# Attention decode with a gated MLP on one core: K evacuation on one engine, 32-column score matmuls, running maxima, one K stream with V trailing, deeper buffers

## The chip, the cores and the metric

One core of a Trainium2 chip (trn2). Times are microseconds (us) of device time; medians over the executions of a kernel. Ratios are the mean time of one kernel's fast runs over that of the other's from the same rounds on the same chip, so they are not quite the ratios of the medians that stand beside them.

## The reference, cut to what matters

```python
# x: 1x1x1024; k_cache, v_cache: 1x4x65536x128 (bf16); 32 query heads, 8 per K/V head
q = (x @ wq)                                    # wq 1024x4096
p = softmax(q k^T / sqrt(128)); o = p v         # over 65536 positions, 4 K/V heads
a = o @ wo                                      # wo 4096x1024
z = gelu(x @ w_in); ...; b = (z1 * g) @ w_out   # w_in 1024x3584, w_out 1792x1024
out = g * a + (1 - g) * b                       # 1x1x1024
```

K and V are 67 MB each. All the rest that is read is 28 MB. Every byte is used once, so the kernel reads 162 MB and does little arithmetic on each.

## The kernel before

K arrives in blocks of 4096 positions (1 MB), one transfer each, as [128 partitions, 2, 2048]: on every partition two runs of 4096 bytes. TensorE transposes 8 chunks of 128x128 into a PSUM tile; VectorE and ScalarE in turn copy it to a staging tile; TensorE multiplies it with 8 query columns; VectorE copies 64 chunks of scores into one big SBUF tile. When a head is done, VectorE takes its maximum, ScalarE does the exponentials in place, and V blocks are multiplied with them. (SBUF is the large on-chip memory that the transfers fill, PSUM the one that TensorE writes; an evacuation is a copy out of PSUM; QK is the product of keys and queries, a chunk is 128 positions of it, and a bank is one PSUM tile of scores.)

```python
KN_BUFS = 4; V_BUFS = 5; W_BUFS = 4; WO_BUFS = 2; STG_BUFS = 4
...
cpool, apool, spool, wpool, kpool, vpool, wopool, stpool   # SBUF pools, opened in this order
...                                                        # (each pool follows the one before it)
S_all = spool.tile([P, Hkv, NA, REP, 8], BF16, name="S_all")
...
class KHead:
    def emit_block(self, b, eng):                          # eng is nc.sync
        knat = rr(kpool, "k", KN_BUFS, [P, NSB, R * Dh], BF16)
        eng.dma_start(out=knat[:], in_=A_k_cache[...].rearrange("(sbl p r) d -> p sbl (r d)", p=P, r=R))
        for ...:                                           # 4 groups of 8 transposes
            pt = rr(ppt, "t", PT_BUFS, [P, 8, P], BF16)
            ...                                            # nc.tensor.transpose x8
            if evac_ctr[0] % 2 == 0: nc.vector.tensor_copy(out=stg[:], in_=pt[:])
            else:                    nc.scalar.copy(out=stg[:], in_=pt[:])
            evac_ctr[0] += 1
            ...                                            # QK of the group two back
...
def softmax_stats(g):
    Mg = apool.tile([P, REP], F32, name=f"M{g}")           # 32 bytes per partition, one for each head
    nc.vector.tensor_reduce(out=Mg[:], in_=S_all[:, g]..., op=ALU.max)
...
for g in range(1, Hkv):                                    # head by head
    for b in range(lead): kh.emit_block(b, eng)            # 4 K blocks alone
    softmax_exp(g - 1)
    for b in range(lead, NBLK):                            # 12 pairs of a K and a V block
        kh.emit_block(b, eng); vh.emit_block(vb_idx, eng)
        if vb_idx == wo_at: vh.emit_wo(nc.scalar)          # 2 MB of output weights, ScalarE's queue
        ...
    ...                                                    # 4 V blocks alone, output projection
```

A scheduler orders the instructions of each engine; the order here is close to the one written.

## Time and profile before

Median 424.48 us of 4 runs.

The page's table of 40 slices (10.5 us each), of the kernel before: busy tenths of engines, granted TensorE clock in tenths, mean busy tenths of the 16 DMA engines, and GB/s moved.

```profile
PE   0224998899887998868868888959878888673443
DVE  0001433444654334353433333354332333510000
ACT  1000434455559434516624333436432333250000
PEclk9999859699969769975988887757885888855555
DMA  7999999999989999999999999999999999999991
GB/s 257 412 410 366 418 411 413 399 401 401 372 328 386 407 408 407 406 408 407 399 393 410 406 409 407 409 408 391 404 373 409 405 409 406 407 393 408 408 379 54
```

The DMA is busy from end to end and moves about 407 GB/s, with small dips at the fourth slice (366), at 105 to 126 us (372, 328) and at 305 us (373).

The chain of waits of the kernel before, shares by engine: DMA first.

```profile
DMA 49%; PE 37%; DVE 5%; ACT 4%; issue 2%; SPq 2%; ACTq 0%
```

The groups of instructions that the change touches, before (busy us and mean ns of one behind the count; then idle time before them and what ended it):

```profile
L284 ACT COPY stg<-t 128x1024 bf16<-128x1024 bf16 x128 | 129.0, 1012 | 188.9 <-PE t L274 186.3
L282 DVE COPY stg<-t 128x1024 bf16<-128x1024 bf16 x128 | 88.3, 690 | 126.6 <-PE t L274 125.7
L254 DVE CAST S_all<-qk 128x512 bf16<-128x512 f32 x32 | 22.1, 692 | 38.5 <-PE qk L246 38.2
L299 DVE TENSOR_REDUCE M<-S_all 128x8 f32<-128x4096 bf16 x4 | 17.7, 4417 | 0.1
```

The waits of the DMA queue's own engine (SPq is SyncE's sequencer, which issues K, V and most weights), before; us in total, times, longest.

```profile
SPq L263 <- PE t L274: 115.9, 44, 6.2
SPq L346 <- DMA wo<-in_A_wo_dram: 21.9, 2, 11.0
SPq L133 <- DMA wo<-in_A_wo_dram: 14.5, 1, 14.5
SPq L154 <- DMA wo<-in_A_wo_dram: 13.5, 1, 13.5
```

The first line: the issue of a K block waits for a free K buffer, which is what limits run-ahead. The other three: the issue of query weights, input weights and V waits for the landing of *output* weights. Such sums are time in which SyncE stood still, not time lost: that has to be read from what the DMA did meanwhile.

### The profile page before, as it was taken

The page shows a single profiled execution, that of the slowest core. Times are in us where ns is not written, and L with a number is a line of the kernel's source. Part 1 is how long each engine was busy: PE and PEld are TensorE (multiplying, and loading weights), DVE is VectorE, ACT ScalarE, POOL GpSimd, SP SyncE. Part 2 cuts the span into 40 slices and gives each one's busy share as a digit, 9 for nine tenths or more (in the row PEclk, how much of TensorE's full clock was granted, in tenths as well). Part 3 has the DMA queues.
Part 4 walks back from the last instruction along what each step waited for, and adds up shares of the span by engine and source line. Part 5 has one row for each costly group of instructions (what it writes and reads, how often), then busy time and mean ns, then how long its engine had stood idle before and what let it go on. Part 6 is the DMA issues. An engine that isn't in the chain of part 4 may idle for free.

```text
span 420.6 us, 15057 instructions
## 1 busy us (share of the span) xinstructions
PE 312.6 (74%) x7018; PEld 295.9 (70%) x7018; DVE 138.9 (33%) x232; ACT 156.2 (37%) x198; POOL 2.4 (1%) x12
## 2 busy tenths in 40 slices
PE   0224998899887998868868888959878888673443
PEld 0224898788777997868868877949878888573333
DVE  0001433444654334353433333354332333510000
ACT  1000434455559434516624333436432333250000
POOL 2000000000000000000000000000000000000000
PEclk9999859699969769975988887757885888855555
DMA  7999999999989999999999999999999999999991
GB/s 257 412 410 366 418 411 413 399 401 401 372 328 386 407 408 407 406 408 407 399 393 410 406 409 407 409 408 391 404 373 409 405 409 406 407 393 408 408 379 54
DMA packets 43583, 162.99 MB, mean 388 GB/s; under 512 B 2816, under 2 KB 2816, under 8 KB 42496
## 3 DMA queue, kind: packets, MB, share of 16 engines
q1 hardware_dynamic: 39072, 153.63, 92.3%
q10 hardware_dynamic: 4160, 8.39, 5.4%
q8 instruction: 55, 0.90, 0.9%
q0 software_dynamic: 288, 0.00, 0.1%
q14 instruction: 8, 0.07, 0.0%
HBM read 162.01 MB, written 0.00 MB: 385 GB/s over the span
## 4 chain that ended last, share of the span: by engine, by line
DMA 49%; PE 37%; DVE 5%; ACT 4%; issue 2%; SPq 2%; ACTq 0%
DMA k<-in_A_k_cache_dram 31%; PE t L274 22%; DMA v<-in_A_v_cache_dram 11%; DMA w<-in_A_wq_dram 8%; PE qk L246 6%; PE acc L355 5%; DVE M L299 3%; ACT S_all L320 2%; ACT stg L284 2%; PE outa_ps L388 1%; SPq L346 1%; DVE S_all L254 1%; PE acc L136 0%; SPq L263 0%; PE nm_ps L312 0%
## 5 line engine op out<-in xcount | busy, mean ns | idle before, releaser
L284 ACT COPY stg<-t 128x1024 bf16<-128x1024 bf16 x128 | 129.0, 1012 | 188.9 <-PE t L274 186.3
L274 PE MATMUL t<-ident_b,k 128*128 128x128 bf16 x2048 | 179.3, 254 | 24.9 <-DMA k<-in_A_k_cache_dram 21.5
L274 PEld LDWEIGHTS <-k 128*128 128x128 bf16 x2048 | 150.5, 115 | 27.9 <-DMA k<-in_A_k_cache_dram 23.5
L282 DVE COPY stg<-t 128x1024 bf16<-128x1024 bf16 x128 | 88.3, 690 | 126.6 <-PE t L274 125.7
L355 PE MATMUL acc<-S_all,v 128*128 128x8 bf16 x2048 | 65.3, 175 | 31.7 <-DMA v<-in_A_v_cache_dram 27.8
L246 PE MATMUL qk<-qT,stg 128*128 128x8 bf16 x2048 | 85.6, 168 | 4.3 <-ACT stg L284 2.4
L355 PEld LDWEIGHTS <-v 128*128 128x128 bf16 x2048 | 60.4, 100 | 34.5 <-DMA v<-in_A_v_cache_dram 30.0
L246 PEld LDWEIGHTS <-stg 128*128 128x128 bf16 x2048 | 74.4, 100 | 12.7 <-ACT stg L284 6.5
L254 DVE CAST S_all<-qk 128x512 bf16<-128x512 f32 x32 | 22.1, 692 | 38.5 <-PE qk L246 38.2
L320 ACT ACTIVATE S_all<-S_all,nm 128x512 bf16<-128x512 bf16 x32 | 22.6, 710 | 23.1 <-DVE nm L314 23.1
L136 PE MATMUL acc<-xT,w 128*128 128x1 bf16 x256 | 8.1, 166 | 23.5 <-DMA w<-in_A_wq_dram 23.5
L136 PEld LDWEIGHTS <-w 128*128 128x128 bf16 x256 | 7.4, 104 | 24.1 <-DMA w<-in_A_wq_dram 24.1
L299 DVE TENSOR_REDUCE M<-S_all 128x8 f32<-128x4096 bf16 x4 | 17.7, 4417 | 0.1
L379 DVE TENSOR_TENSOR oT_sb<-acc,rl 128x8 bf16<-128x8 f32 x4 | 0.7, 167 | 44.2 <-PE acc L355 44.2
L303 PE MATMUL mT_ps<-ident_f,M 128*8 128x128 f32 x4 | 1.4, 351 | 11.6 <-DVE M L299 11.6
L146 DVE TENSOR_TENSOR qT_acc<-qT_acc,acc 128x32 f32<-128x32 f32 x7 | 1.3, 188 | 23.9 <-PE acc L136 23.9
L303 PEld LDWEIGHTS mT_ps<-ident_f,M 128*8 128x8 f32 x4 | 0.3, 83 | 12.1 <-DVE M L299 12.1
L388 PEld LDWEIGHTS <-wo 128*128 128x128 bf16 x256 | 7.5, 104 | 1.5 <-issue 1.5
L388 PE MATMUL outa_ps<-oT_sb,wo 128*128 128x1 bf16 x256 | 7.5, 165 | 1.1 <-DVE oT_sb L379 1.0
L157 PE MATMUL acc<-xT,w 128*128 128x1 bf16 x224 | 6.8, 164 | 0.0
L157 PEld LDWEIGHTS <-w 128*128 128x128 bf16 x224 | 6.3, 98 | 0.0
L320 ACT ACTIVATION_READ_ACCUMULATOR S_all<-S_all,nm 128x1 f32 x32 | 6.0, 188 | 0.0
(64 smaller groups left out, 36.5 us busy)
## 6 DMA issues: line engine op xcount, KB each, us to landing
k<-in_A_k_cache_dram SPq DMA_DIRECT2D x64, 1024.0 KB, 15.0
v<-in_A_v_cache_dram SPq DMA_DIRECT2D x64, 1024.0 KB, 14.8
wo<-in_A_wo_dram ACTq DMA_DIRECT2D x4, 2048.0 KB, 18.9
w<-in_A_wq_dram SPq DMA_DIRECT2D x8, 1024.0 KB, 13.6
w<-in_B_w_in_dram SPq DMA_DIRECT2D x8, 896.0 KB, 16.3
w<-in_B_w_out_dram SPq DMA_DIRECT2D x7, 512.0 KB, 13.2
x<-in_A_x_dram SPq DMA_DIRECT2D x1, 2.0 KB
g<-in_gate_w_dram SPq DMA_DIRECT2D x1, 2.0 KB
```

The source lines that it names most:

```text
L136: nc.tensor.matmul(qps[:, h : h + 1], lhsT=wqb[:, h * Dh : (h + 1) * Dh], rhs=xT[:, dc : dc + 1], start=True, stop=True,)
L157: nc.tensor.matmul(zps[:, fi : fi + 1], lhsT=wib[:, fi * P : (fi + 1) * P], rhs=xT[:, dc : dc + 1], start=True, stop=True,)
L246: nc.tensor.matmul(self.qkb[:, cl, :], lhsT=stg[:, j, :], rhs=qT[:, g * REP : (g + 1) * REP], start=True, stop=True,)
L254: nc.vector.tensor_copy(out=S_all[:, g, bank * (CPB // 8) : (bank + 1) * (CPB // 8), :, :], in_=self.qkb[:].rearrange("p (a b) h -> p a h ...
L274: nc.tensor.transpose(out=pt[:, j, :], in_=knat[:, sbl, r * Dh : (r + 1) * Dh], identity=ident_b[:],)
L282: nc.vector.tensor_copy(out=stg[:], in_=pt[:])
L284: nc.scalar.copy(out=stg[:], in_=pt[:])
L299: nc.vector.tensor_reduce(out=Mg[:], in_=S_all[:, g].rearrange("p a h b -> p h a b"), axis=AX.XY, op=ALU.max)
L320: nc.scalar.activation(out=S_all[:, g, :, h, :], in_=S_all[:, g, :, h, :], func=ACT.Exp, bias=nmg[:, h : h + 1], scale=SCALE, accum_out=L[ ...
L346: eng.dma_start(out=vb[:], in_=A_v_cache[0, g, b * BROWS : (b + 1) * BROWS, :].rearrange("(sbl p r) d -> p sbl (r d)", p=P, r=R),)
L355: nc.tensor.matmul(self.oT_ps[:, :REP], lhsT=vb[:, sbl, r * Dh : (r + 1) * Dh], rhs=S_all[:, g, c // 8, :, c % 8], start=(c == 0), stop=(c ...
L388: nc.tensor.matmul(outa_ps[:, jn : jn + 1], lhsT=wo_tiles[gg][:, h, jn * P : (jn + 1) * P], rhs=oT_sb[:, gg * REP + h : gg * REP + h + 1], ...
```

## The change

The intent is to take ScalarE out of the K path, to give TensorE wider score matmuls and longer runs of one kind, to spread the maximum of each head over its blocks, to run K as one stream of 64 blocks with V trailing by 22, and to have more buffers. The diff, cut to its core:

```diff
-KN_BUFS = 4
-V_BUFS = 5
+KN_BUFS = 5
+V_BUFS = 6
-STG_BUFS = 4
+STG_BUFS = 6
-PT_BUFS = 3
-QK_SKEW = 2          # groups of 8 chunks
-K_LEAD = 4
+PT_BUFS = 4
+QK_SKEW = 1          # blocks
+K_LEAD = 6
...
-    CPB = 64
+    NQK_W = NQ
+    CPB = 512 // NQK_W                      # 16 chunks in a bank of scores
...
+    Mrun = apool.tile([P, Hkv, REP], F32, name="Mrun")
+                        mb = apool.tile([P, REP], F32, name="mb", tag="mb", bufs=2)
-        Mg = apool.tile([P, REP], F32, name=f"M{g}")
+    oT_accs = apool.tile([P, Hkv, REP], F32, name="oT_accs")
...
-                    rhs=qT[:, g * REP : (g + 1) * REP],
+                    rhs=qT[:, :NQK_W],      # 32 columns, 8 of them used
...
-                    if evac_ctr[0] % 2 == 0:
-                        nc.vector.tensor_copy(out=stg[:], in_=pt[:])
-                    else:
-                        nc.scalar.copy(out=stg[:], in_=pt[:])
+                    nc.vector.tensor_copy(out=stg[:], in_=pt[:])
...                   # V sums per block in PSUM, added up in oT_accs; one accumulator bank, not two
-    (head by head: 4 K blocks, 12 pairs, 4 V blocks)
+    for i in range(NKTOT):                  # 64 K blocks
+        kheads[g].emit_block(b, eng)
+        ...
+        if i - OFFSET >= 0: emit_v_global(i - OFFSET)      # OFFSET = 22
...
-                vh.emit_wo(nc.scalar)
+            vh.emit_wo(nc.sync)
```

More of the change, by code (lines that the diff above doesn't have):

```diff
@@ L67 @@
     NCH = Sk // P
-    CPB = 64
+    NQK_W = NQ
+    PVW = 8
+    CPB = 512 // NQK_W
     assert NCH % CPB == 0
@@ L72 @@
     assert CPBLK % 8 == 0
-    assert NCH % 8 == 0
-    NA = NCH // 8
     cpool = ctx.enter_context(tc.tile_pool(name="cpool", bufs=1))
@@ L133 @@
         nc.sync.dma_start(out=wqb[:, : NQ * Dh], in_=A_wq[dc * P : (dc + 1) * P, :])
-        qps = rr(pacc, "acc", 2, [P, max(NZC, NQ)], F32)
+        qps = rr(pacc, "acc", 1, [P, max(NZC, NQ, PVW * REP)], F32)
         for h in range(NQ):
@@ L154, in emit_win_block @@
         eng.dma_start(out=wib[:, :F], in_=B_w_in[dc * P : (dc + 1) * P, :])
-        zps = rr(pacc, "acc", 2, [P, max(NZC, NQ)], F32)
+        zps = rr(pacc, "acc", 1, [P, max(NZC, NQ, PVW * REP)], F32)
         for fi in range(NZC):
@@ L220 @@
     uT_holder = {}
+    NA = NCH // 8
     S_all = spool.tile([P, Hkv, NA, REP, 8], BF16, name="S_all")
+    spad = spool.tile([P, 256], BF16, name="spad")
+    nc.gpsimd.memset(spad[:], 0.0)
     L = apool.tile([P, Hkv, REP], F32, name="L")
+    Mrun = apool.tile([P, Hkv, REP], F32, name="Mrun")
     rl_tiles = [None] * Hkv
@@ L244, in emit_qk_bank @@
                 if cl == 0:
-                    self.qkb = rr(psqk, "qk", QK_BANK_BUFS, [P, CPB, REP], F32)
+                    self.qkb = rr(psqk, "qk", QK_BANK_BUFS, [P, CPB, NQK_W], F32)
                 nc.tensor.matmul(
@@ L253, in emit_qk_bank @@
                 if cl == CPB - 1:
+                    c0 = bank * (CPB // 8)
+                    c1 = (bank + 1) * (CPB // 8)
                     nc.vector.tensor_copy(
-                        out=S_all[:, g, bank * (CPB // 8) : (bank + 1) * (CPB // 8), :, :],
-                        in_=self.qkb[:].rearrange("p (a b) h -> p a h b", b=8),
-                    )
+                        out=S_all[:, g, c0:c1, :, :],
+                        in_=self.qkb[:, :, g * REP : (g + 1) * REP].rearrange(
+                            "p (a b) h -> p a h b", b=8
+                        ),
+                    )
+                    if bank == 0:
+                        nc.vector.tensor_reduce(
+                            out=Mrun[:, g, :],
+                            in_=S_all[:, g, c0:c1].rearrange("p a h b -> p h a b"),
+                            axis=AX.XY,
+                            op=ALU.max,
+                        )
+                    else:
+                        mb = apool.tile([P, REP], F32, name="mb", tag="mb", bufs=2)
+                        nc.vector.tensor_reduce(
+                            out=mb[:],
+                            in_=S_all[:, g, c0:c1].rearrange("p a h b -> p h a b"),
+                            axis=AX.XY,
+                            op=ALU.max,
+                        )
+                        nc.vector.tensor_tensor(
+                            out=Mrun[:, g, :], in0=Mrun[:, g, :], in1=mb[:], op=ALU.max
+                        )
                 self.c_qk += 1
@@ L268, in emit_block @@
             )
+            blk_pending = []
             for sbl in range(NSB):
@@ L280, in emit_block @@
                     stg = rr(stpool, "stg", STG_BUFS, [P, 8, P], BF16)
-                    if evac_ctr[0] % 2 == 0:
-                        nc.vector.tensor_copy(out=stg[:], in_=pt[:])
-                    else:
-                        nc.scalar.copy(out=stg[:], in_=pt[:])
+                    nc.vector.tensor_copy(out=stg[:], in_=pt[:])
                     evac_ctr[0] += 1
-                    self.pending.append((stg, 8))
-                    if len(self.pending) > QK_SKEW:
-                        p_stg, n = self.pending.pop(0)
-                        self.emit_qk_bank(p_stg, n)
+                    blk_pending.append((stg, 8))
+            self.pending.append(blk_pending)
+            while len(self.pending) > QK_SKEW:
+                for p_stg, n in self.pending.pop(0):
+                    self.emit_qk_bank(p_stg, n)
         def flush(self):
             while self.pending:
-                p_stg, n = self.pending.pop(0)
-                self.emit_qk_bank(p_stg, n)
+                for p_stg, n in self.pending.pop(0):
+                    self.emit_qk_bank(p_stg, n)
             assert self.c == NCH and self.c_qk == NCH
     def softmax_stats(g):
-        Mg = apool.tile([P, REP], F32, name=f"M{g}")
-        nc.vector.tensor_reduce(
-            out=Mg[:], in_=S_all[:, g].rearrange("p a h b -> p h a b"), axis=AX.XY, op=ALU.max
-        )
         mT_ps = pm.tile([REP, P], F32, name=f"mT_ps{g}", tag="m")
-        nc.tensor.transpose(out=mT_ps[:], in_=Mg[:], identity=ident_f[:])
+        nc.tensor.transpose(out=mT_ps[:], in_=Mrun[:, g, :], identity=ident_f[:])
         mx8 = apool.tile([REP, 1], F32, name=f"mx8_{g}")
@@ L337, in __init__ @@
             self.c = 0
-            self.oT_ps = None
+            self.nblk = 0
         def emit_block(self, b, eng):
             g = self.g
-            if self.oT_ps is None:
-                self.oT_ps = rr(pacc, "acc", 2, [P, max(NZC, NQ)], F32)
-                oT_tiles[g] = self.oT_ps
+            oT_ps = rr(pacc, "acc", 1, [P, max(NZC, NQ, PVW * REP)], F32)
             vb = rr(vpool, "v", V_BUFS, [P, NSB, R * Dh], BF16)
@@ L351, in emit_block @@
             )
+            first = True
             for sbl in range(NSB):
@@ L354, in emit_block @@
                     c = self.c
+                    last = (sbl == NSB - 1 and r == R - 1)
                     nc.tensor.matmul(
-                        self.oT_ps[:, :REP],
+                        oT_ps[:, : REP],
                         lhsT=vb[:, sbl, r * Dh : (r + 1) * Dh],
                         rhs=S_all[:, g, c // 8, :, c % 8],
-                        start=(c == 0),
-                        stop=(c == NCH - 1),
+                        start=first,
+                        stop=last,
                     )
+                    first = False
                     self.c += 1
+            if self.nblk == 0:
+                nc.vector.tensor_copy(out=oT_accs[:, g, :], in_=oT_ps[:, :REP])
+            else:
+                nc.vector.tensor_tensor(
+                    out=oT_accs[:, g, :], in0=oT_accs[:, g, :], in1=oT_ps[:, :REP], op=ALU.add
+                )
+            self.nblk += 1
         def emit_wo(self, eng):
@@ L380, in out_proj @@
             out=oT_sb[:, gg * REP : (gg + 1) * REP],
-            in0=oT_tiles[gg][:, :REP],
+            in0=oT_accs[:, gg, :],
             in1=rl_tiles[gg][:],
@@ L414, in emit_wout_block @@
         )
-        obps = rr(pacc, "acc", 2, [P, max(NZC, NQ)], F32)
+        obps = rr(pacc, "acc", 1, [P, max(NZC, NQ, PVW * REP)], F32)
         for jn in range(NOC):
@@ L433 @@
     vheads = [VHead(g) for g in range(Hkv)]
+    NKTOT = Hkv * NBLK
+    OFFSET = NBLK + K_LEAD
     NWOB = FC // FPB
@@ L437, with emit_v_global @@
     wout_left = list(range(NWOB))
-    for b in range(NBLK):
-        kheads[0].emit_block(b, eng)
+    wo_at = min(2, NBLK - 1)
+    def emit_v_global(j):
+        g, b = divmod(j, NBLK)
+        vh = vheads[g]
+        vh.emit_block(b, eng)
+        if b == wo_at:
+            vh.emit_wo(nc.sync)
+        if b == NBLK - 1:
+            assert vh.c == NCH
+            out_proj(g)
+    for i in range(NKTOT):
+        g, b = divmod(i, NBLK)
+        kheads[g].emit_block(b, eng)
+        if b == NBLK - 1:
+            kheads[g].flush()
+            softmax_stats(g)
+            softmax_exp(g)
         if win_left:
@@ L445 @@
             emit_wout_block(wout_left.pop(0), eng)
+        j = i - OFFSET
+        if j >= 0:
+            emit_v_global(j)
     while win_left:
@@ L451 @@
         emit_wout_block(wout_left.pop(0), eng)
-    kheads[0].flush()
-    softmax_stats(0)
-    wo_at = min(2, NBLK - 1)
-    for g in range(1, Hkv):
-        kh = kheads[g]
-        vh = vheads[g - 1]
-        lead = min(K_LEAD, NBLK)
-        for b in range(lead):
-            kh.emit_block(b, eng)
-        softmax_exp(g - 1)
-        vb_idx = 0
-        for b in range(lead, NBLK):
-            kh.emit_block(b, eng)
-            vh.emit_block(vb_idx, eng)
-            if vb_idx == wo_at:
-                vh.emit_wo(nc.scalar)
-            vb_idx += 1
-        kh.flush()
-        softmax_stats(g)
-        while vb_idx < NBLK:
-            vh.emit_block(vb_idx, eng)
-            if vb_idx == wo_at:
-                vh.emit_wo(nc.scalar)
-            vb_idx += 1
-        assert vh.c == NCH
-        out_proj(g - 1)
-    softmax_exp(Hkv - 1)
-    vh = vheads[Hkv - 1]
-    for b in range(NBLK):
-        vh.emit_block(b, eng)
-        if b == wo_at:
-            vh.emit_wo(nc.scalar)
-    assert vh.c == NCH
-    out_proj(Hkv - 1)
+    for j in range(max(0, NKTOT - OFFSET), NKTOT):
+        emit_v_global(j)
     diff = apool.tile([P, NOC], F32, name="diff")
```

## The prediction

> **What bounds the kernel now.** The DMA. The page's table of slices and the table of stretches show 400 to 415 GB/s from 10 us to 407 us of a 420.6 us span; 163 MB at the 407 GB/s of the K/V stages is about 400 us of the span. The Trainium skill ("Perfetto Trace Analysis", Roofline) bounds one core by its 16 DMA engines at about 435 GB/s; this trace's best stretch is 420. Time in which the DMA is not saturated, from 5 us stretches: about 3 us at the start; 0.7 us at 35-40; about 2 us at 110-130 (the DMA falls to 25-160 GB/s at 121-123: four K-only blocks after the weights run out, plus a 4.4 us VectorE maximum that stops TensorE); 0.7 us at 305-310 (waits on K and V issue); and about 13 us from 407 on, where the last V block lands at 413.9 and 5 us of output projection and epilogue follow. TensorE (74% busy), VectorE (33%) and ScalarE (37%) are not bounds, except briefly.
>
> **What the change does.** Bytes are unchanged. K evacuations all go to VectorE: 256 x 0.690 us = 177 us (now 88 there, and 129 on ScalarE). Score evacuations become 128 of 128x128 instead of 32 of 128x512 (0.692 us): estimate 0.29 us each from 0.157 us fixed + 1.04 ns per element, 37 us. The four 4.42 us maxima become 128 of about 0.28 us plus as many 0.16 us combines, 57 us. V sums add 64 x 0.165 = 11 us. VectorE: about 139 -> 290 us, 69%. ScalarE keeps only the exponentials. QK streams 32 columns instead of 8; pitch now is 33 ns warm and 51 ns cold, and I expect no change, since weight loads set it. K is one 64-block stream with V 22 blocks behind: one K-only run of 7 blocks instead of three of 4, and a V-only tail of 22 blocks.
>
> **On the critical path.** VectorE per K/V pair: 4 x 0.69 + 2 x 0.73 + 0.17 = 4.4 us, against 5.15 us of DMA: it fits. TensorE per pair, from warm and cold stretches of the timeline: 3.8 us warm, 5.9 us cold. The kernel's mean clock is 0.79, so compute averages about 5.0 us per pair: the margin shrinks, since warm pairs are now paced by VectorE (4.4), not by TensorE (3.8). The Trainium skill ("TensorE: Matmul & The Clock Gate", Part 4) says transposes don't count as activity for the clock; this trace agrees in that the clock recovers during QK, V and weight matmuls after as much as 14 us of nearly unbroken transposes at half clock. The new order puts 32 transposes in a row, so cold spells may grow.
> Gains: the maxima's stall and two of three K-only leads, 2 to 3 us. Losses: in the output-weight blocks (3.9 us of DMA) and the K-only run (2.6 us) VectorE needs 4.2 to 4.4, a lag of about 15 us that five K buffers just about absorb; I allow 0 to 5 us. The tail is the same.
>
> **Predicted:** 424.5 us, 8 in 10 between 416 and 440. Faster by over 2%: 0.08; within 2%: 0.68; slower by over 2%: 0.24.
>
> **What would show it.** DMA near 407 GB/s from 130 us to 5 us before the last landing; VectorE near 290 us busy; QK pitch unchanged; no long VectorE maximum; a dip, if any, at 95-130 us; the last 22 V blocks at 2.6 us each; the chain of waits again mostly DMA.
>
> **What would make it wrong.** A clock that stays at 0.5 through the pairs (5.9 us x 42 pairs, +30 us); VectorE's in-order queue holding K evacuations behind waits for QK or V, so that pairs exceed 5.15 us; or DMA engines that run faster with deeper buffers (faster than I think possible).

## More of the kernel before

The kernel before has a median between 423.1 and 425.1 us, depending on the job, so small differences are read from the ratios.

Where a tile lies in SBUF follows from the sizes of all tiles in the pools before it.

## The result, and the profile after

The kernel after takes 409.78 us (409.18 to 410.56, 10 runs) against 424.04 us: ratio 0.9664, 95% interval 0.9643 to 0.9685. That is faster by 3.4%, and outside the range of 416 to 440 us.

The page's slices (10.2 us each) of the kernel after:

```profile
PE   1349888988997888899995888888948887553444
DVE  0018787999999787588684878687657875100001
ACT  1000002000500000230000000500000001400000
PEclk9999896999998888789786988698687887555555
DMA  6999999999999999999999999999999999999981
GB/s 239 419 419 424 417 423 413 412 414 417 368 418 412 415 419 417 419 419 417 416 413 419 417 419 417 416 418 419 413 404 418 419 416 410 379 412 421 420 348 43
```

The DMA engines were busy before and are busy now, yet they move 417 GB/s instead of 407 in nearly every slice of the K and V stages, and in the V-only tail. (The first slices, of query weights, are higher too, 419 instead of 412 and 410, but the address is not the reason there: e3 below, with the old addresses and one queue, has 421 in its second slice.) On 162 MB, 407 against 417 GB/s is 9.5 us (162,000/407 - 162,000/417). The dip at slice 4 is gone, and that of 105 us is one slice (368) instead of two and a half.

The same in stretches of 30 us (length, then busy us and count of PE, PEld, DVE, ACT and POOL, clock, DMA busy share, GB/s). The kernel before:

```profile
135.00:165.00 30.00, 29.29 (x661) 28.29 (x659) 11.65 (x17) 14.22 (x15) 0.00 (x0) 0.77 1.03 409
225.00:255.00 30.00, 25.21 (x545) 24.14 (x543) 9.40 (x14) 10.84 (x12) 0.00 (x0) 0.83 1.03 408
```

and the kernel after:

```profile
135.00:165.00 30.00, 25.27 (x571) 24.37 (x570) 23.49 (x66) 0.00 (x0) 0.00 (x0) 0.84 1.02 416
225.00:255.00 30.00, 25.70 (x594) 24.60 (x590) 24.61 (x71) 0.00 (x0) 0.00 (x0) 0.88 1.02 418
```

Same busy share of the DMA engines, 2% more bytes. So each packet should take less time; engines that wait less would show a higher share.

The chain of waits and the groups after:

```profile
DMA 63%; PE 18%; DVE 15%; issue 2%; SPq 0%; ACT 0%; ACTq 0%
```

```profile
L308 DVE COPY stg<-t 128x1024 bf16<-128x1024 bf16 x256 | 165.7, 683 | 39.5 <-PE t L301 38.9
L260 DVE CAST S_all<-qk 128x128 bf16<-128x128 f32 x128 | 35.5, 284 | 2.7 <-PE qk L250 2.5
L275 DVE TENSOR_REDUCE mb<-S_all 128x8 f32<-128x128 bf16 x124 | 33.3, 281 | 2.4
L281 DVE TENSOR_TENSOR Mrun<-Mrun,mb 128x8 f32<-128x8 f32 x124 | 19.9, 161 | 1.9
```

VectorE's work came out as predicted in kind and a little smaller (258.5 us, 63% of the span; predicted 290). None of the waits of SyncE's queue names the output weights any more; the longest in total is

```profile
SPq L289 <- PE qk L250: 59.5, 26, 9.3
```

The trace also records every DMA packet (one contiguous piece of a transfer). For the 32,768 packets of 4096 bytes (all of K and V) the records give:

```
kernel   median ns   middle half   95th percentile   share at exactly 159 ns   mean of those up to 180 ns
before      162       159 to 165         169                 26%                      162.58
after       159       159 to 159         159                 99%                      159.01
```

(Under 1% of the packets in either kernel take over 180 ns; they are left out of the mean.) Before, packets are spread over 159 to 171 ns; after, 99% take 159. The difference of the means is 2.2%, and the gain in GB/s, 409 to 416 and 408 to 418 above, is of that size.

What could change the time of a packet? The sources in memory, the transfers and their sizes are the same. Four things differ. The change made some small tiles of the pool *ahead* of the large ones bigger: four maxima of 32 bytes went (128 bytes), and a 128-byte running maximum, two 32-byte scratch tiles and a 128-byte sum came, 192 bytes more. (Behind the score tile it also has an unused tile of 512 bytes, `spad`, which the cut diff leaves out; 512 is a multiple of 256.) In the built programs the weight, K and V buffers start at bytes 54,080, 86,848 and 119,616 of each partition before: all 64 past a multiple of 256. After, they start at 54,784, 87,552 and 128,512: all multiples of 256. The second is that the output weights moved from ScalarE's queue to SyncE's, so that one queue is left; the third that more transfers are in flight; the fourth that ScalarE is idle and the order is new.

The Trainium skill ("DMA: Bandwidth & Descriptors", How a descriptor splits into AXI transactions) says that a transfer is cut into transactions of 256 bytes that start at multiples of 256, so that one which starts off such a boundary costs additional beats. That is a reason to suspect the address; but the page words it for reading (bytes that are "fetched but unused") and does not say whether it holds for the writing side. The experiments decide.

### The profile page after: what moved, and what is told of

Read it like the earlier page. It is cut to its first block, busy times and chain, and to the rows that moved or that the text cites. A ratio compares the mean times of both kernels' runs of the same rounds, so it can differ in the third digit from the quotient of the medians.

```text
span 408.6 us, 15215 instructions
## 1 busy us (share of the span) xinstructions
PE 305.9 (75%) x7018; PEld 291.1 (71%) x7018; DVE 258.5 (63%) x768; ACT 27.5 (7%) x70; POOL 2.7 (1%) x13
## 4 chain that ended last, share of the span: by engine, by line
DMA 63%; PE 18%; DVE 15%; issue 2%; SPq 0%; ACT 0%; ACTq 0%
DMA k<-in_A_k_cache_dram 44%; DMA v<-in_A_v_cache_dram 14%; DVE stg L308 10%; PE t L301 9%; DMA w<-in_A_wq_dram 5%; PE acc L378 3%; PE qk L250 3%; DVE mb L275 1%; DVE S_all L260 1%; PE outa_ps L419 1%; DVE Mrun L281 1%; PE acc L136 1%; ACT L204 0%; PE lb_ps L406 0%; PE nm_ps L333 0%
## 5 line engine op out<-in xcount | busy, mean ns | idle before, releaser
L308 DVE COPY stg<-t 128x1024 bf16<-128x1024 bf16 x256 | 165.7, 683 | 39.5 <-PE t L301 38.9
L301 PE MATMUL t<-ident_b,k 128*128 128x128 bf16 x2048 | 161.4, 250 | 29.0 <-DMA k<-in_A_k_cache_dram 28.1
L301 PEld LDWEIGHTS <-k 128*128 128x128 bf16 x2048 | 148.0, 114 | 33.4 <-DMA k<-in_A_k_cache_dram 30.9
L250 PE MATMUL qk<-qT,stg 128*128 128x32 bf16 x2048 | 79.5, 180 | 11.0 <-DVE stg L308 9.4
L250 PEld LDWEIGHTS <-stg 128*128 128x128 bf16 x2048 | 67.8, 99 | 16.5 <-DVE stg L308 15.7
L390 DVE TENSOR_TENSOR oT_accs<-oT_accs,acc 128x8 f32<-128x8 f32 x60 | 9.7, 162 | 56.7 <-PE acc L378 56.0
L260 DVE CAST S_all<-qk 128x128 bf16<-128x128 f32 x128 | 35.5, 284 | 2.7 <-PE qk L250 2.5
L275 DVE TENSOR_REDUCE mb<-S_all 128x8 f32<-128x128 bf16 x124 | 33.3, 281 | 2.4
L281 DVE TENSOR_TENSOR Mrun<-Mrun,mb 128x8 f32<-128x8 f32 x124 | 19.9, 161 | 1.9
## 6 DMA issues: line engine op xcount, KB each, us to landing
w<-in_A_wq_dram SPq DMA_DIRECT2D x8, 1024.0 KB, 10.2
```

The lines of the kernel that those rows point to most:

```text
L250: nc.tensor.matmul(self.qkb[:, cl, :], lhsT=stg[:, j, :], rhs=qT[:, :NQK_W], start=True, stop=True,)
L260: nc.vector.tensor_copy(out=S_all[:, g, c0:c1, :, :], in_=self.qkb[:, :, g * REP : (g + 1) * REP].rearrange("p (a b) h -> p a h b", b=8),)
L275: nc.vector.tensor_reduce(out=mb[:], in_=S_all[:, g, c0:c1].rearrange("p a h b -> p h a b"), axis=AX.XY, op=ALU.max,)
L281: nc.vector.tensor_tensor(out=Mrun[:, g, :], in0=Mrun[:, g, :], in1=mb[:], op=ALU.max)
L301: nc.tensor.transpose(out=pt[:, j, :], in_=knat[:, sbl, r * Dh : (r + 1) * Dh], identity=ident_b[:],)
L390: nc.vector.tensor_tensor(out=oT_accs[:, g, :], in0=oT_accs[:, g, :], in1=oT_ps[:, :REP], op=ALU.add)
```

## The experiments

Theory: the address of the DMA's destinations. Rivals: queue, depth, order, evacuation, columns. Eighteen kernels were run, all correct. Each edit is against the kernel named first.

### Move the buffers, nothing else

e1, the kernel before with a dead tile; the order of instructions on each engine is the same but for its memset:

```diff
+    apad = spool.tile([P, 96], BF16, name="apad")      # 192 bytes
+    nc.gpsimd.memset(apad[:], 0.0)
     S_all = spool.tile([P, Hkv, NA, REP, 8], BF16, name="S_all")
```

> The kernel before with one unused 192-byte-per-partition tile in front of the score tile, so that all DMA destination buffers start at a multiple of 256 bytes (before: 64 bytes past one); order of instructions unchanged. Alignment theory (the DMA writes of the old layout cost extra time per packet): 4096-byte packets go from a spread of 159 to 171 ns to a uniform 159 ns, DMA in the saturated stretches from 406 to 417 GB/s, time about 414 us (410 to 417). Rivals (one DMA queue instead of two, deeper buffers, new schedule, idle ScalarE): 424 us, packets unchanged.

Measured: 416.62 us (415.01 to 417.99), ratio 0.980 (0.977 to 0.983). Packets: 99% at 159 ns.

e2, the kernel after with the same tile of 64 bytes (`[P, 32]`), which puts its buffers 64 bytes past a multiple of 256:

> The kernel after with one unused 64-byte-per-partition tile in front of the score tile, so that the DMA destinations start 64 bytes past a multiple of 256, as in the kernel before. Alignment theory: packets spread over 159 to 171 ns again, about 406 GB/s, time about 420 us (417 to 423). Rivals: 410 us, packets stay at 159 ns.

Measured: 419.88 us (419.71 to 420.88), ratio 0.988 against the kernel before; packets spread again, mean 162.67 ns.

The slices' GB/s of e1, then of e2:

```profile
GB/s 250 413 424 339 404 422 420 413 409 401 319 301 337 416 419 416 417 417 418 413 418 414 420 416 420 417 418 372 413 416 418 417 419 417 419 372 397 419 420 100
```

```profile
GB/s 242 419 413 415 411 411 402 401 401 405 361 411 397 405 409 407 407 409 407 406 397 407 407 409 406 406 407 406 402 395 409 406 407 403 398 387 411 408 318 34
```

A dead tile of 192 bytes takes the old kernel from 407 to 417 GB/s; one of 64 bytes takes the new kernel back to 407. The address is the cause of the higher rate. But e1 is not at 410: with the faster DMA its dips are *deeper* (339 in slice 4, and 319, 301, 337 at 104 to 135 us, where the kernel before has 372, 328, 386). There, the transfers are not short of bandwidth, they are not issued. So about 7 us are left to explain.

### The rivals, alone

e3, `vh.emit_wo(nc.scalar)` to `vh.emit_wo(nc.sync)` in the kernel before; e4, `KN_BUFS` 4 to 5 and `V_BUFS` 5 to 6 in the kernel before. Both leave the buffers 64 bytes off.

> The kernel before with the output-projection weights loaded from the SyncE queue instead of the ScalarE queue, layout unchanged. Queue theory (two DMA queues in turn cost time per packet): packets go to a uniform 159 ns, 417 GB/s, time about 414 us. Alignment theory: packets unchanged, 421 to 426 us.

> The kernel before with 5 K and 6 V buffers instead of 4 and 5, destinations still 64 bytes past a multiple of 256. Depth theory (more transfers in flight keep the DMA engines faster): 417 GB/s, about 414 us. Alignment theory: 406 GB/s and the same packet times; at most the dip at 110 to 130 us and the stall at 305 to 310 us shrink, 420 to 425 us.

Measured: e3 423.55 us, ratio 0.996 (0.993 to 0.999); e4 423.08 us, ratio 0.995 (0.992 to 0.998); packets as before in both (means 162.62 and 162.87 ns). Neither sets the rate. Each is worth half a per cent alone: so e3, in which SyncE no longer waits for output weights, gains about 2 us of the 50 us of such waits.

### How the address counts

e5, e6 and e7 are the kernel after with dead tiles of 32, 128 and 256 bytes. e8 moves only the DMA's destinations: 64 bytes ahead of the weight buffers and 192 bytes ahead of the staging tiles, so that the score tile and the staging tiles, which only engines write, stay at multiples of 256:

```diff
+    wpad = wpool.tile([P, 32], BF16, name="wpad")      # first in its pool
+    tpad = stpool.tile([P, 96], BF16, name="tpad")     # first in its pool
```

> The kernel after with all DMA destinations moved by 32 bytes (32 past a multiple of 256). If a DMA write needs only 32-byte beats to be whole: 410 us and 159 ns packets. If it needs 64-byte or larger units: packets of 160 to 175 ns, 419 to 424 us (an offset of 64 gave 419.9).

> The same moved by 128 bytes. If the unit is 256 bytes: about 420 us as with 64 bytes. If the unit is 128 bytes: 410 us and uniform packets.

> The same moved by 256 bytes: control that moving as such costs nothing. If the unit is 256 bytes or less: 409 to 411 us, 159 ns packets. If the unit is 512 bytes, or the old addresses were lucky in another way: about 420 us.

> The kernel after with only the DMA destinations (weights, K, V, output weights) moved by 64 bytes; the score tile and the staging tiles, which engines write, stay at multiples of 256. If the cost sits in the DMA writes: about 420 us, as when everything moved. If it sits in the engines' accesses of the score and staging tiles: 410 us.

```
run                     DMA destinations mod 256    us (median)    mean packet up to 180 ns
after                              0                  409.78              159.01
e5                                32                  420.21              162.80
e2                                64                  419.88              162.67
e6                               128                  419.10              162.72
e7                                 0 (moved by 256)   410.98              159.02
e8 (DMA only)                     64                  419.63              162.74
```

It is a step, not a slope: any of the three offsets costs 3.7 to 3.8 ns on a packet, and 256 bytes cost nothing. The unit is 256 bytes, and the cost is in the DMA's writes (e8), not in what engines read or write. Why such a write takes longer was not shown, and other offsets were not tried. Nor does it hold for every packet: the medians of the after kernel and of e2 are 84 and 86 ns for 2048 bytes, 272 and 275 ns for 7168 bytes (input weights), but 309 ns in both for the 8192 bytes of the query weights.

### What is left: buffers, queue, or the new code

e9 is e1 with 5 K and 6 V buffers. e10 to e12 undo one part of the kernel after each: every second evacuation on ScalarE again (e10), 8 query columns and with them banks of 64 chunks (e11), the old order, head by head (e12). All have aligned buffers.

```diff
 # e10                                            # e11
-    nc.vector.tensor_copy(out=stg[:], in_=pt[:]) -    NQK_W = NQ
+    if evac_ctr[0] % 2 == 0: nc.vector...        +    NQK_W = REP
+    else: nc.scalar.copy(out=stg[:], in_=pt[:])  -    rhs=qT[:, :NQK_W]
                                                  +    rhs=qT[:, g * REP : (g + 1) * REP]
```

> The aligned kernel before (416.6 us, with DMA dips at 35-40, 105-135 and 285-295 us) with 5 K and 6 V buffers. If the buffers carry the rest of the gain: 410 to 412 us and no dips. If the new order carries it: 414 to 417 us.

> The kernel after with every second K evacuation on ScalarE again. If VectorE alone paces the blocks from 70 to 125 us, as its 5.0 of 5 us there say, the dip of the DMA to 349 GB/s at 105-110 us goes: 407 to 410 us. If the one-engine evacuation is itself part of the gain (no waits on ScalarE): 411 to 415 us.

> The kernel after with 8 query columns per score matmul as before, banks of 64 chunks and so score evacuations of 128x512 and maxima of 512 elements. If the 32 columns keep TensorE's clock up: clock below 0.78 and 412 us or more. If they are waste: clock about 0.80, fewer VectorE us (about 235), 407 to 410 us.

> The kernel after with the old order of emission (three K-only leads of 4 blocks, V of a head finished before the next head's pairs). If the single 64-block K stream with V 22 blocks behind carries the rest of the gain: 413 to 418 us with dips after each head. If not: 409 to 411 us.

Measured: e9 413.96 us (ratio 0.976), e10 410.22 us (0.968), e11 412.70 us (0.974), e12 409.54 us (0.966). e9 fits neither of its expectations, 410 to 412 us or 414 to 417. The order (e12) and the evacuation on one engine (e10) carry no part of the gain: undoing either changes the time by 0.5 us at most. (In e10 the dip at 105 to 110 us goes, 414 GB/s instead of 349, but one of 306 comes at 110 to 115.) e11 does lose 3 us, as its first alternative said, and its clock is lower (0.779 against 0.809). e9 has a new hole in the 21st slice (315; e4, with the same buffers and queues, has 257 there):

```profile
GB/s 256 411 424 344 395 422 419 414 414 415 412 411 381 418 417 418 416 417 419 414 315 387 418 417 418 419 420 414 413 406 416 420 418 418 418 417 418 419 387 46
```

The queue's waits of e9 between 195 and 220 us say why:

```profile
SPq L348 <- DMA wo<-in_A_wo_dram: 13.5, 1, 13.5
```

SyncE did not issue a V block for 13.5 us because of a load of output weights on ScalarE's queue. V does not need those weights. The built program shows the link. It has eight completion counters for the transfers of both queues and deals them out in turn (that is how this program was built, not a rule of the chip); before a counter is given to a new transfer, the issuing engine waits for the old one to land. Of the kernel before:

```
queue     transfer      waits for counter      raises
ScalarE   wo0 (1st)     -                      DMAHW0
SyncE     w0 (5th wq)   DMAHW3, DMAHW0         DMAHW0
...
ScalarE   wo0 (3rd)     DMAHW5, DMAHW0         DMAHW5
...
SyncE     v3            DMAHW5                 DMAHW5
```

On one queue a counter comes back after seven younger transfers, in the order in which they were issued. On two, ScalarE issues when it gets there (at 0.7 us two of the four loads, ahead of nearly all query weights), the order of landings is no longer the order of issue, and SyncE stands still for a stranger's 2 MB. At the start that is the dip in the fourth slice, which is gone in every kernel with one queue. No run kept two queues with counters of their own, so that the counter is what costs the time, and not when the weights are loaded, is read from the waits and from the program, not tested alone.

### One part at a time, on the old code

After these runs it was open what carries the rest. e13 is the kernel after with 8 columns but its small banks (`NQK_W = REP`, `CPB = 16`); e14 is e9 with the output weights on SyncE's queue (`nc.scalar` to `nc.sync`); e15 is e14 with 32 columns and banks of 16 chunks; e16 tries to beat both kernels; e17 and e18 complete the set.

> The kernel after with 8 query columns but its small banks of 16 chunks, so that score evacuations and maxima stay 128x128. If the extra columns themselves help (TensorE's clock): clock about 0.78 and 412 to 413 us, as with 8 columns and large banks. If the small banks help: 409 to 411 us and clock about 0.81.

> The kernel before, aligned, with 5 K and 6 V buffers, and the output weights on SyncE's queue. The dip of the DMA at 31 to 42 us (344 GB/s with the weights on ScalarE's queue, where two of the four loads run at the start; 414 in the misaligned kernel with them on SyncE) should go: 411 to 412.5 us, from 414.0. If the queue does nothing here: 413.5 to 414.5 us.

> The same with 32 query columns and banks of 16 chunks, evacuations still on two engines, old maxima, old order. If columns or banks are the last large part: 409 to 411 us and clock about 0.80. If not: no different from the run before it, within 1 us.

> The kernel after with one output-weight buffer instead of two (loaded with V block 9 instead of 2), and the space given to a fifth weight buffer and a seventh V buffer. If the dips at 5-10 us (303 GB/s, four weight buffers) and at 345-350 us (333 GB/s, V buffers full) come from too few buffers: 407.5 to 409 us. If not: 409.5 to 410.5 us.

> The kernel before, aligned, output weights on SyncE's queue, still 4 K and 5 V buffers. If the queue alone carries the last part: 409 to 411 us. If buffers and queue are both needed: 412 to 415 us, with dips of the DMA where the K-only leads run out of buffers (105 to 135 us).

> The kernel before with 5 K and 6 V buffers and the output weights on SyncE's queue, but destinations 64 bytes past a multiple of 256 as they were. If alignment is worth about 10 us whatever the rest: 418 to 421 us, like the kernel after when it is misaligned (419.9), with packets spread over 159 to 171 ns.

The three parts on the code of the kernel before, all eight combinations; the ratio is to the kernel before in the same rounds:

```
aligned   5 K, 6 V buffers   wo on SyncE   run      us       ratio
  no            no               no        before   424.04   1
  no            no               yes       e3       423.55   0.996
  no            yes              no        e4       423.08   0.995
  no            yes              yes       e18      419.65   0.992
  yes           no               no        e1       416.62   0.980
  yes           no               yes       e17      415.39   0.982
  yes           yes              no        e9       413.96   0.976
  yes           yes              yes       e14      409.25   0.965
the kernel after                                    409.78   0.966
the kernel after, 64 bytes off             e2       419.88   0.988
```

e14 is the kernel before with three small edits, and it has the whole gain. What it was expected to give, 411 to 412.5, was too cautious. The GB/s of e17 and of e14 show that buffers and queue are needed together:

```profile
GB/s 241 418 421 422 420 420 411 414 410 344 311 381 418 416 417 417 417 419 356 417 410 419 420 416 419 417 409 265 414 411 418 417 419 419 417 413 418 419 419 79
```

```profile
GB/s 229 418 422 420 425 419 411 414 416 416 407 410 418 417 419 415 418 418 418 417 412 419 416 420 418 419 418 377 411 416 420 416 420 416 417 403 419 421 349 53
```

With 4 and 5 buffers (e17) the fourth slice is whole, but the K-only leads of the three later heads (slices 10 to 12, 19 and 28) run out of buffers: 344, 311, 356, 265. With the deeper buffers (e14) they nearly vanish. With deeper buffers and two queues (e9) the waits for output weights take the buffers' run-ahead away again; in e14 no wait of SyncE's queue names the output weights.

e13, 410.51 us (409.80 to 411.25), settles e11: 8 columns with small banks cost some 0.7 us, no more than the intervals of the two ratios, though the clock is at 0.768 instead of 0.809. In e15 the 32 columns raise the clock of e14 from 0.769 to 0.802, and the time is 409.06 against 409.25 us. (e15 changes the banks too; e13 against the kernel after changes the columns alone.) So wider matmuls do keep TensorE's clock up, and here that buys next to nothing, for TensorE is not what bounds the kernel. The other 2 us of e11 came with its large banks (on the old code, e14 against e15, large banks cost nothing). Its profile shows a DMA at 307 GB/s from 95 to 105 us where e13 has 399, with TensorE 9.15 us busy of 10 at a clock of 0.83 (e13: 8.98 at 1.00); what of that was the bank size and what a cold spell that fell there was not separated.

e16, a fifth weight buffer and a seventh V buffer in the place of one output-weight buffer, gave 409.25 us (408.94 to 411.67): the dip at 345 to 350 us goes (419 GB/s), that at 5 to 10 us stays (302), and the time is the same. No version was clearly faster than the kernel after: e14, e15, e16 and the kernel after lie within 0.2%.

## Why the prediction was wrong

**"163 MB at the 407 GB/s of the K/V stages": the step that failed.** The bytes are unchanged, as it said. But the prediction took the rate of the saturated DMA for a constant and wrote that a change of it would need DMA engines "that run faster with deeper buffers (faster than I think possible)". The rate depends on where the buffers lie. Moving those of the kernel before by 192 bytes took it to 417 GB/s (e1), and moving those of the kernel after by 64 took it back to 407 (e2). The aligned and the misaligned kernel after are 10.1 us apart (419.88 - 409.78), of a gain of 14.3. The diff shows the cause only as a few bytes of small tiles, which no reading of engines, waits and overlaps would have weighed; the addresses in the built program would have shown it. The prediction even had a clue that the rate is no constant: this trace's best stretch was 420 GB/s, in the query weights, whose 8192-byte packets the address does not slow.

**"Gains: ... 2 to 3 us. Losses: ... I allow 0 to 5 us": the term that was mis-sized.** The misaligned kernel after (e2, ratio 0.988) is 1.2% faster than the kernel before, some 5 us, where the sum said 0 net. The gain was larger and its reason another. The prediction credited the shorter maxima and the fewer K-only leads; e12 has the old leads and is as fast (409.54 us), and e14 has the old maxima too (409.25 us). Most of what gained was the deeper buffers with the single queue (e18, ratio 0.992, without any of the new code); what is between 0.992 and 0.988 is within the two intervals. The move of the output weights, one word in the diff, was not costed at all, although the waits of the queue's own engine show 50 us (21.9 + 14.5 + 13.5) of SyncE standing for a load of output weights.

**The lag of VectorE.** The loss allowed for it came to about 1 us: at 100 to 110 us the DMA falls to 394 and 349 GB/s. The prediction took 4.2 to 4.4 us per block; back to back, four evacuations take 2.40 us (0.60 each, not the 0.69 of one alone), and a block of the output-weight stage took 3.8 us and one of the K-only run 3.3. These lines of the chain of waits of the kernel after (start, duration, what) show the period of the former:

```profile
77.95 2.40 DVE stg L308 x4
81.76 2.40 DVE stg L308 x4
85.56 2.40 DVE stg L308 x4
```

**The clock.** The prediction also expected that cold spells (stretches at half clock) may grow, because the new order puts 32 transposes in a row. It rested this on the Trainium skill ("TensorE: Matmul & The Clock Gate", Part 4), which says that a transpose does not count as TensorE being busy in the way that other matmuls do, and it said that this trace agrees. The trace says the opposite, and the measurement decides. The mean clock of the profiled run went up, from 0.787 to 0.809. In the trace of the kernel before, the granted clock changes in steps of 3.41 us (its records begin at 43 us). The 20 steps at half clock that were followed by full clock hold 24 to 31 transposes each and only 8 to 28 other matmuls; those followed by half clock hold 0 to 24 transposes and up to 101 others. One can also count the columns that the matmuls of a step stream (128 in a transpose, 8 in a V matmul, 8 or 32 in a QK matmul, 1 in one with weights): in the kernels before and after, each step that is followed by full clock holds at least 2944, and each that is followed by half clock at most 3136. So here transposes count, and by this count, which fits two traces and was not tested by a run of its own, 32 columns instead of 8 should help too; in the runs they lift the clock by 0.03 to 0.04 (e13, e15). The pitch of QK matmuls (start to start) did not change, as predicted: a median of 25 ns at full clock and 27 ns at half, before and after (the prediction's 33 and 51 ns are too large).

**What was right.** That the kernel is bound by the DMA before and after, though the rate it names for afterwards, 407 GB/s, is not the one measured; that VectorE's load (predicted about 290 us, measured 258.5, 63% of the span) fits, but for the 1 us above; the sizes of the new VectorE instructions (284, 281 and 161 ns against 0.29, 0.28 and 0.16 us); that the tail would not change (the last V block lands 6.7 us before the end before, 6.8 us after); and that a dip would stand at 95 to 130 us.

## What to carry to other kernels

Where a kernel is bound by its transfers, look at the addresses of the buffers they write before anything else: a pool whose small tiles do not add up to a multiple of 256 bytes moves every large buffer behind it. Here, with most bytes in packets of 4096, that cost 1.4 to 2.7% of the time in the five pairs of runs that differ in it (1.4 with one queue and shallow buffers, 2.7 with one queue and deep ones), with nothing in any wait to show for it. Compare GB/s at equal busy share, and the times of single packets, to tell a slower transfer from a late one. Then read who the *issuing* engine waits for: a transfer on a second queue can hold up the first through a shared counter, and here deeper buffers gave their full worth only when that was gone; three small edits then did as much as a rewrite.

## What the Trainium skill lacked or had wrong

- "DMA: Bandwidth & Descriptors", How a descriptor splits into AXI transactions: that destinations in SBUF should start at multiples of 256 bytes is not said (the page speaks of the bytes that a transaction reads), nor what it costs. Here: 4096-byte packets 159 ns aligned, 162.7 to 162.8 ns on average at offsets 32, 64 and 128, that is 417 against 407 GB/s, while packets of 8192 bytes take 309 ns either way. If its rule held for writes, the size would not fit either: by an estimate worked out from it, a 4096-byte run at offsets of 32, 64 and 128 needs 129, 130 and 132 beats instead of 128, a cost that grows with the offset (0.8, 1.6 and 3.1%); measured, it is 2.3 to 2.4% at each.
- "DMA: Bandwidth & Descriptors", Issuing engines are not separate DMA queues, says that a second issuing engine only saves the time to issue. In a program that deals out its completion counters to both queues it can also cost time: with aligned, deeper buffers, moving four 2 MB loads to the one queue took 413.96 to 409.25 us (e9, e14), and the main queue's waits for them, up to 14.8 us, were gone. No page warns that a counter shared by two queues can keep one of them from issuing.
- "TensorE: Matmul & The Clock Gate" does not say that the width of small matmuls counts for the clock: 32 columns for 8 raised the mean granted clock from 0.768 to 0.809 (e13 against the kernel after) and from 0.769 to 0.802 (e14 against e15), at no cost in time. Its Part 4, on transposes that don't count as busy, is not borne out here: half clock gave way to full clock only after steps of 3.41 us with 24 to 31 transposes in the kernel before.
